# A fused attention and mixer kernel: all tasks put in the order of a precomputed table, the last two weight transfers held behind early loads, batch four's rk by DMA transpose, uT in two tiles

## The chip, the cores and the metric

One Trainium2 chip, one core. The metric is the device time of one execution in microseconds (us). An execution over 1.5% above the fastest of the same kernel is called slow and is left out of ratios. Each kernel was profiled in one execution only, so a trace shows what can happen, not always what happens each time. The profile gives the span from the first to the last instruction, 1.0 to 1.8 us below the time.

Names: PE is TensorE (matmuls and transposes by matmul), ACT is ScalarE, DVE is VectorE, POOL is GpSimd, SP is SyncE, here only a queue that issues transfers. The kernel is written so that each engine takes its instructions in the order in which they were emitted.

## The reference

A linear attention with decay over B=4 batches, H=8 heads, S=768 steps, D=48, then a token and channel mixer:

```python
for t in range(S):                                       # attention, per batch and head
    cur = einsum('bhd,bhe->bhde', u[None] * kt, vt)
    y[:, :, t] = einsum('bhd,bhde->bhe', rt, state + cur)
    state = w[None, :, :, None] * state + einsum('bhd,bhe->bhde', kt, vt)
x = y.transpose(0, 2, 1, 3).reshape(B, S, H * D)         # (4, 768, 384)
h = relu(x.T @ w_tok1) @ w_tok2                          # token mixer, 768 -> 256 -> 768
u = x + h.T
out = u + relu(u @ w_ch1) @ w_ch2                        # channel mixer, 384 -> 1536 -> 384
```

## The kernel before

The 768 steps of a batch are cut into 6 units of 128 steps. A unit goes through: loads of k, r, v (192 KB each, on SP's queue); kp = k times decay, rp = r times decay; transposes of both (rk); scores `at`; masked scores `AT`; state `kv`; output `y`; sum `x_b`. Batch one, for which there is no other work to overlap with, uses an f32 form (`m`, `trk`, `trr`, `mT`, `ad`) with more PE and less POOL work. When a batch's six `x_b` are there, its mixer runs: `hidden`, `back` (u_sb), a transpose of u (uT), 24 `up` steps (z_ps, zr) and 6 `down` steps (h_ps, osb), of which each `up` is 3 matmuls of 384 columns and each `down` 12. The next batch's attention is meant to run beside this batch's mixer.

Order is written out by hand: in batch one slot by slot, later by weaving lists with guessed costs.

```python
def load_unit(b, c):                                   # SP's queue, k then r then v
    for nm, src in (("kt", k), ("rt", r), ("vt", v)):
        ...
        ins = sp.dma_start(dst, src[b, :, ts(c, T), :].rearrange("h s d -> s h d"))
        if (b, c) in after and nm == "kt":             # (1, 0): wait for batch one's last x_b
            tc.add_manual_dep(ins.ins, after[b, c].ins.name, ..., reason="weights first")
...
WEIGHTS_AT = {4: (0,), 5: (1,), 6: (2,), 7: (3, 4)}    # POOL's queue, by slot of batch one;
                                                       # 2 and 3 are the halves of w_ch1, 4 is w_ch2
WARM = (10, 2, 1)                                      # idle_ps matmuls to keep PE's clock up:
                                                       # 10 at the start, then 2 or 1 a slot
...
after[1, 0] = done[0, C - 1]
...                                                    # batch one's mixer beside batch two's attention
items = ups(0, 0, 6) + u1[:6] + downs(0, 0, 0, 1) + u1[6:] + downs(0, 0, 1) + downs(0, 1)
events = [att(0.5, 6), att(4.0, 7)] + [att(8.0 + 3.2 * j, 8 + j) for j in range(7)] + mixing(...)
merge(items, fetch([0.0] * 6 + [12.0, 15.0, 18.0, 22.0, 35.0, 36.5]) + events)
```

rk of batches two to four is turned on PE (8 matmuls into PSUM) and copied by ACT. u of batches two to four is turned by DMA into one tile `uT` of 3 x 768.

Of the kernel before, what the change touches and what calls it, by code (L numbers as in the profile page):

```python
# [18 lines left out]
Ln = ACTF.Ln  # L19


@with_exitstack
def kernel(
# [24 lines left out]
    NJ = dch // 128  # L48

    const = ctx.enter_context(tc.tile_pool(name="const", bufs=1))  # L50
    wts = ctx.enter_context(tc.tile_pool(name="wts", bufs=1))
    lpool = ctx.enter_context(tc.tile_pool(name="lpool", bufs=8))
# [3 lines left out]
    zpool = ctx.enter_context(tc.tile_pool(name="zpool", bufs=2))  # L56
# [4 lines left out]


# [11 lines left out]


    loaded = {}
    done = {}
    after = {}

    rpads = [const.tile([128, H, P], f32, name=f"rpad{c}") for c in range(C)]  # L80

    def load_unit(b, c):
        tiles = []
        for nm, src in (("kt", k), ("rt", r), ("vt", v)):
            if b == 0 and nm == "rt":
                t = rpads[c]
                dst = t[:, :, 0:D]
            else:
                t = lpool.tile([128, dm], f32, name=nm)
                dst = h3(t)  # L90
            ins = sp.dma_start(dst, src[b, :, ts(c, T), :].rearrange("h s d -> s h d"))
            if (b, c) in after and nm == "kt":
                tc.add_manual_dep(ins.ins, after[b, c].ins.name,
                                  mybir.DependencyInfo(mybir.DependencyClass.Sync,
                                                       mybir.DependencyReason.DATA),
                                  reason="weights first")
            tiles.append(t)
        loaded[b, c] = tiles



# [5 lines left out]
    act.dma_start(w_bc, w.rearrange("h d -> (h d)").partition_broadcast(128))  # L107
# [5 lines left out]
    load_unit(0, 0)  # L113
    sp.dma_start(ud, u.rearrange("h d -> (h d)").rearrange("(j p) -> p j", p=128))
    load_unit(0, 1)
# [4 lines left out]
    WARM = (10, 2, 1)  # L120

    def keep_warm(n):

        for _ in range(n):
            z_ps = psM.tile([128, 512], f32, name="idle_ps", tag="m")
            pe.matmul(z_ps, warm[:, 0:128], warm, start=True, stop=True)

# [32 lines left out]
    NB = 3  # L160
    rps = []; kps = []; S0s = []
    for i in range(NB):
        kp_i = const.tile([128, H, P], bf16, name=f"kp{i}")
        dve.memset(kp_i, 0.0)
        kps.append(kp_i)

    keep_warm(WARM[0])
# [5 lines left out]
    wpT = const.tile([128, G, HP, T], f32, name="wpT")  # L173

# [6 lines left out]
    def decay_rT(g):  # L181
        if g == 0:
            for a in range(HP):
                act.activation(wpT[:, g, a, :], steps[:, ts(g, T)], Exp, scale=lnwd[:, a:a + 1])
        else:
            act.activation(wpT[:, g], powers[g - 1], Exp)

    powers = [const.tile([128, HP, T], f32, name=f"powers{g}") for g in range(1, G)]

    def exponents(g):  # L190
        pool.tensor_mul(powers[g - 1], steps[:, ts(g, T)].unsqueeze(1).to_broadcast([128, HP, T]),
                        lnwd.unsqueeze(2).to_broadcast([128, HP, T]))
# [3 lines left out]
    wG = const.tile([128, HP], f32, name="wG")  # L196
    decay_rT(0)
    u_blk = const.tile([128, 3, H], f32, name="u_blk")


    for i in range(2):
        S_i = const.tile([128, HP, 2, D], bf16, name=f"S0_{i}")
        S0s.append(S_i)
    bm = const.tile([128, HP, 2, D], f32, name="bm")
    wGm = const.tile([128, HP, 2, D], f32, name="wGm")


# [8 lines left out]
    def constants_1():  # L216
        pool.tensor_mul(u_blk, heads, ud.unsqueeze(2).to_broadcast([128, 3, H]))

    def constants_2():
        act.activation(wG, lnwd, Exp, scale=float(G * T))  # L220
        pool.tensor_mul(wGm, bm, wG.unsqueeze(2).unsqueeze(3).to_broadcast([128, HP, 2, D]))

    def constants_3():

        for i in range(NB):
            rp_i = const.tile([128, H, P], bf16, name=f"rp{i}")
            dve.memset(rp_i, 0.0)
            rps.append(rp_i)


# [3 lines left out]
    wch2 = wts.tile([128, NJ, dm], bf16, name="wch2")  # L234

    WEIGHTS_AT = {4: (0,), 5: (1,), 6: (2,), 7: (3, 4)}

    def load_weights(which):
        half = ds(0, dch // 2), ds(dch // 2, dch // 2)
        parts = [(wtok1, moe_w_tok1), (wtok2, moe_w_tok2), (wch1[0], moe_w_ch1[:, half[0]]),  # L240
                 (wch1[1], moe_w_ch1[:, half[1]]), (wch2, moe_w_ch2)]
        for i in which:
            t, src = parts[i]
            pool.dma_start(t, src.rearrange("(c p) k -> p c k", p=128))

    x_bs = [xpool.tile([128, C, dm], bf16, name="x_b", bufs=3) for b in range(B)]


    live = {}
    kv = [None]  # L250
    count = [0]

    BY_POOL = (3, 5)

    def stage_p(b, c):

        g = c % G
        kt, rt, vt = loaded.pop((b, c))
        i = count[0] % NB
        count[0] += 1  # L260
        kp = kps[i]
        vb = apool.tile([128, dm], bf16, name="vb", bufs=4)
        L = live[b, c] = dict(kp=kp, vb=vb, rt=rt, vt=vt)
        (dve if b == 0 and c not in BY_POOL else pool).tensor_mul(kp[:, :, 0:D], h3(kt), h3(wn[:, g, :]))
        if b == 0:
            L["m"] = apool.tile([128, dm], f32, name="m", bufs=2)
            pool.tensor_mul(h3(L["m"]), h3(kt), rt[:, :, 0:D])
        if b > 0:
            L["rp"] = rps[i]
            pool.tensor_mul(L["rp"][:, :, 0:D], h3(rt), h3(wp[:, g, :]))  # L270
            L["ku"] = apool.tile([128, dm], f32, name="ku", bufs=2)
            pool.tensor_mul(L["ku"], kt, u_bc)

# [3 lines left out]
    def stage_a(b, c):  # L277

        L = live[b, c]
        rk = L["rk"] = apool.tile([128, 2, HP, T], bf16, name="rk")  # L280
        if b == 0:

            trk = psM.tile([128, HP, T], bf16, name="trk", tag="m")
            trr = psM.tile([128, HP, T], f32, name="trr", tag="m")
            for a in range(HP):
                pe.transpose(trk[:, a, :], pair(L["kp"], a), ident)
            act.copy(rk[:, 0], trk)
            for a in range(HP):
                pe.transpose(trr[:, a, :], pair(L["rt"], a), ident_f)
            dve.tensor_mul(rk[:, 1], trr, wpT[:, c % G])  # L290
            mT_ps = psM.tile([128, 3, T], f32, name="mT_ps", tag="m")
            for j in range(3):
                pe.transpose(mT_ps[:, j, :], L["m"][:, ts(j, 128)], ident_f)
            L["mT"] = apool.tile([128, 3, T], f32, name="mT", bufs=2)
            act.copy(L["mT"], mT_ps)
            act.copy(L["vb"], L["vt"])
            return
        tr_ps = psM.tile([128, 2, HP, T], bf16, name="tr_ps", tag="m")
        for j, src in ((0, L["kp"]), (1, L["rp"])):
            for a in range(HP):  # L300
                pe.transpose(tr_ps[:, j, a, :], pair(src, a), ident)
        act.copy(rk, tr_ps)
        act.copy(L["vb"], L["vt"])

        rku = apool.tile([128, dm], f32, name="rku", bufs=2)
        dve.tensor_mul(rku, L["ku"], L["rt"])
        L["adg"] = apool.tile([128, H], f32, name="adg")
        dve.tensor_reduce(L["adg"], h3(rku), axis=mybir.AxisListType.X, op=ALU.add)

    def own_step(L):  # L310
        L["yd"] = apool.tile([128, dm], f32, name="yd")
        pool.tensor_mul(h3(L["yd"]), h3(L["vb"]), L["adg"].unsqueeze(2).to_broadcast([128, H, D]))

    def stage_b(b, c):

        L = live[b, c]
        rk = L["rk"]
        if b > 0:
            own_step(L)
        at_ps = [psA.tile([128, HP, T], f32, name=f"at_ps{q}", tag=f"at{q}") for q in range(2)]  # L320
        for a in range(HP):
            for q in range(2):
                rows = slice(q * P, q * P + D)
                pe.matmul(at_ps[q][:, a, :], rk[rows, 0, a, :], rk[rows, 1, a, :], start=True, stop=True)
        L["AT"] = []
        for q in range(2):
            AT = apool.tile([128, HP, T], bf16, name=f"AT{q}")
            dve.tensor_mul(AT, at_ps[q], mask.unsqueeze(1).to_broadcast([128, HP, T]))
            L["AT"].append(AT)
        if b == 0:  # L330

            ad_ps = psM.tile([128, H], f32, name="ad_ps", tag="m")
            for j in range(3):
                pe.matmul(ad_ps, L["mT"][:, j, :], u_blk[:, j, :], start=(j == 0), stop=(j == 2))
            L["adg"] = apool.tile([128, H], f32, name="adg")
            act.copy(L["adg"], ad_ps)

    state = {}

    def stage_c(b, c):  # L340
# [253 lines left out]
```

## Time and profile before

| | before |
|---|---|
| time, median of 3 (range) | 185.08 us (184.67 to 185.6) |
| span of the profiled run | 184.1 us |
| PE busy | 165.5 us, 90% |
| POOL, DVE, ACT busy | 93.8, 106.0, 100.0 us |
| PE idle at 40-50 us | 4.5 us |

From the page of the kernel before: the busy tenths of PE, the granted PE clock and the share of the DMA engines in 40 slices of 4.6 us.

```profile
PE 165.5 (90%) x1504; PEld 106.8 (58%) x1504; DVE 106.0 (58%) x193; ACT 100.0 (54%) x217; POOL 93.8 (51%) x113
...
PE   7788888893699899798999999899999999999992
...
PEclk9999999999699999999999999999999999999999
DMA  4999998999999998124699999233011134211212
```

PE has little to give: 18.6 us of idle in all. The one deep hole is in slices 10 and 11 (counted from one). The DMA engines are full from the second to the sixteenth slice (to about 73 us), so in that time a transfer comes earlier only if another comes later.

The same by windows (columns: window, length, busy us and count per engine, granted clock, DMA share, GB/s):

```profile
30.00:40.00 10.00, 9.26 (x74) 5.40 (x72) 5.01 (x12) 5.62 (x14) 0.83 (x1) 1.00 1.15 183
40.00:50.00 10.00, 5.48 (x32) 3.06 (x30) 1.44 (x2) 4.95 (x11) 4.52 (x5) 0.85 1.10 188
50.00:60.00 10.00, 10.00 (x116) 6.77 (x114) 8.11 (x13) 7.93 (x16) 10.00 (x11) 0.98 1.10 220
```

PE is idle for 4.5 us from 40 to 50 us. POOL (the fifth busy figure) has 0.83 us of work from 30 to 40 us, and is full from 50. What they wait for is in the chain of waits that ended last (start, duration, what):

```profile
32.19 14.15 DMA rt<-in_r_dram
46.48 1.00 POOL rp_661 L68
47.52 0.61 PE tr_ps L68 x4
```

A load of 192 KB, which takes 3.9 us in the median of the page's list of transfers, took 14.15 us here, beside two weight transfers in the same 16 engines: the larger one, issued at 28.46 us, landed 17.6 us later at about 46.1, and r at 46.3. The multiply of r and PE's transpose waited for it:

```profile
43.44 0.40 PE L68 MATMUL tr_ps<-ident,kp_139 128*128 128x128 bf16 x4 [0.83 <-POOL kp_139 L68]
47.52 0.61 PE L68 MATMUL tr_ps<-ident,rp_661 128*128 128x128 bf16 x4 [3.69 <-POOL rp_661 L68]
```

### The profile page before, as it was taken

What the parts mean: (1) busy time and instruction counts of PE and PEld (TensorE: products, weight loads), DVE (VectorE), ACT (ScalarE), POOL (GpSimd) and SP (SyncE); (2) the same over time, 40 slices, a digit from 0 to 9 for tenths busy, and PEclk for the clock granted to TensorE, in tenths of its full rate; (3) what the DMA queues carried; (4) which work ended last, traced back from release to release, by engine and by line L of the source; (5) the groups of instructions that cost most, each with busy time, mean ns of one, the idle gap of its engine ahead of it and who ended that gap; (6) DMA issues with size and microseconds to landing.
All of it is one profiled execution on the core that took longest, in us unless ns stands there. A gap on an engine that the chain in (4) does not pass through costs nothing.

```text
span 184.1 us, 3991 instructions
## 1 busy us (share of the span) xinstructions
PE 165.5 (90%) x1504; PEld 106.8 (58%) x1504; DVE 106.0 (58%) x193; ACT 100.0 (54%) x217; POOL 93.8 (51%) x113
## 2 busy tenths in 40 slices
PE   7788888893699899798999999899999999999992
PEld 2376776461367566465667666666665665656651
DVE  6465877700469999974669977996541071121121
ACT  2695565493578744404959748654645444445500
POOL 5459795002999999943597999991100000000000
PEclk9999999999699999999999999999999999999999
DMA  4999998999999998124699999233011134211212
GB/s 92 185 203 163 191 141 143 196 184 196 187 219 215 234 225 195 45 45 107 136 235 232 189 243 196 44 67 108 0 46 43 43 86 89 85 43 43 85 47 85
DMA packets 90354, 24.44 MB, mean 133 GB/s; under 512 B 83680, under 2 KB 90336, under 8 KB 90336
## 3 DMA queue, kind: packets, MB, share of 16 engines
q1 hardware_dynamic: 86368, 20.85, 54.0%
q0 software_dynamic: 3408, 3.15, 11.0%
q10 hardware_dynamic: 560, 0.20, 0.7%
q8 instruction: 12, 0.20, 0.4%
q14 instruction: 6, 0.05, 0.1%
HBM read 20.84 MB, written 4.72 MB: 139 GB/s over the span
## 4 chain that ended last, share of the span: by engine, by line
PE 58%; POOL 14%; DMA 13%; DVE 6%; ACT 5%; issue 3%; ACTq 0%; SPq 0%; DVEq 0%; POOLq 0%
PE h_ps L68 23%; PE z_ps L68 20%; DMA rt<-in_r_dram 8%; POOL ku L68 3%; POOL yd L68 3%; DMA wd<-in_w_dram 3%; PE tr_ps L68 3%; DMA uT<-u_sb 3%; PE y_ps L68 2%; PE ad_ps L68 2%; POOL rp_661 L68 2%; POOL rp_663 L68 1%; PE hT_ps L68 1%; POOL rp_665 L68 1%; DVE u_sb L68 1%
## 5 line engine op out<-in xcount | busy, mean ns | idle before, releaser
L68 ACT ACTIVATE zr<-z_ps 128x384 bf16<-128x384 f32 x96 | 44.3, 495 | 31.7 <-PE z_ps L68 31.6
L68 PE MATMUL h_ps<-wch_198,zr 128*128 128x384 bf16 x288 | 50.4, 326 | 0.2
L68 PEld LDWEIGHTS <-zr 128*128 128x128 bf16 x288 | 28.0, 98 | 18.9 <-issue 1.0
L68 DVE TENSOR_TENSOR osb<-u_sb,h_ps 128x384 f32<-128x384 bf16 x24 | 13.3, 552 | 44.5 <-PE h_ps L68 44.5
L68 ACT COPY rk<-tr_ps 128x1024 bf16<-128x1024 bf16 x18 | 18.2, 1012 | 19.2 <-PE tr_ps L68 18.7
L68 PE MATMUL z_ps<-uT,wch_0_196 128*128 128x384 bf16 x144 | 27.6, 337 | 1.1 <-DMA uT<-u_sb 1.1
L68 PE MATMUL z_ps<-uT,wch_1_197 128*128 128x384 bf16 x144 | 26.5, 326 | 0.8 <-ACT zr L68 0.6
L68 DVE TENSOR_TENSOR rku<-ku,rt 128x384 f32<-128x384 f32 x18 | 18.6, 1033 | 11.3 <-POOL ku L68 11.3
L68 POOL TENSOR_TENSOR yd<-vb,adg 128x384 f32<-128x384 bf16 x24 | 20.0, 834 | 7.3 <-DVE adg L68 6.7
L68 PEld LDWEIGHTS <-wch_0_196 128*128 128x128 bf16 x144 | 14.0, 101 | 10.4 <-issue 3.2
L68 POOL TENSOR_TENSOR ku<-kt,u_bc 128x384 f32<-128x384 f32 x18 | 20.0, 1110 | 0.0
L68 PEld LDWEIGHTS <-wch_1_197 128*128 128x128 bf16 x144 | 13.8, 98 | 10.1 <-issue 1.7
L68 DVE TENSOR_TENSOR x_b<-y_ps,yd 128x384 bf16<-128x384 f32 x24 | 13.3, 553 | 10.6 <-POOL yd L68 5.6
L68 POOL TENSOR_TENSOR kp_139<-kt,wn 128x384 bf16<-128x384 f32 x7 | 7.0, 999 | 17.2 <-DMA kt<-in_k_dram 11.5
L68 PEld LDWEIGHTS <-rk 48*128 48x128 bf16 (+1 forms) x272 | 11.4, 95 | 6.3 <-issue 3.0
L68 DVE TENSOR_TENSOR u_sb<-x_b,hT_ps 128x384 bf16<-128x384 bf16 x24 | 11.8, 547 | 1.5 <-PE hT_ps L68 1.5
L68 ACT CAST vb<-vt 128x384 bf16<-128x384 f32 x24 | 12.3, 514 | 0.0
L68 DVE TENSOR_REDUCE adg<-rku 128x8 f32<-128x384 f32 x18 | 9.9, 553 | 0.8
L68 PE MATMUL hT_ps<-h1r,wtok_195 128*128 128x384 bf16 x48 | 9.4, 326 | 0.9 <-ACT h1r L68 0.8
L68 PE MATMUL idle_ps<-warm 128*128 128x512 bf16 x20 | 7.8, 520 | 2.2 <-DVE warm L68 1.3
L68 PE MATMUL h_ps<-x_b,wtok_194 128*128 128x384 bf16 x48 | 8.9, 325 | 0.1
L68 POOL TENSOR_TENSOR rp_661<-rt,wp 128x384 bf16<-128x384 f32 x6 | 6.6, 1101 | 3.1 <-DMA rt<-in_r_dram 3.1
(318 smaller groups left out, 253.6 us busy)
## 6 DMA issues: line engine op xcount, KB each, us to landing
kt<-in_k_dram SPq DMA_DIRECT2D x24, 192.0 KB, 3.7
vt<-in_v_dram SPq DMA_DIRECT2D x24, 192.0 KB, 3.9
out_dram<-osb SPq DMA_DIRECT2D x24, 192.0 KB, 1.9
rt<-in_r_dram SPq DMA_DIRECT2D x18, 192.0 KB, 3.9
wch_198<-in_moe_w_ch_dram POOLq DMA_DIRECT2D x1, 1152.0 KB, 17.6
wch_0_196<-in_moe_w_ch_dram POOLq DMA_DIRECT2D x1, 576.0 KB, 8.9
wch_1_197<-in_moe_w_ch_dram POOLq DMA_DIRECT2D x1, 576.0 KB, 10.5
wtok_194<-in_moe_w_tok_dram POOLq DMA_DIRECT2D x1, 384.0 KB, 7.5
```

The costliest lines, as they stand in the source:

```text
L68: return lambda *args, **kw: tc.keep_in_program_order(f(*args, **kw))
```

## The change

The intent: a model of engines and queues, run beforehand, searched for an order of all 900-odd tasks of the kernel; its result is a table of numbers, and the kernel emits task after task by it. With it come: batch two's loads from about 20 us on, not held; the two last weight transfers held behind two k loads; batch four's rk by DMA transpose (SP issues it; no PE, no ACT); two units of batch two in the f32 form; two more kp multiplies on DVE; more warm matmuls in batch one; uT in two tiles; deeper buffers for some tiles, and fewer for the loads (8 to 6). The core of the diff (the table, and the functions that only changed their wrapping, are cut):

```diff
+ORDER = [
+    38, 41, 36, 37, 39, 42, 0, 40, 15, 142, 1, 128, 16, 4, 116, 46, 2, 144, 133, 117, 5, 17, 45, 121, 134,
+    ...                                                        # 914 numbers
+]
+    AHEAD = 6; NB = 4; ZB = 3; RK = 4                          # buffers of loads, kp and rp, zr, rk
+    style = ['f32', ... x6, 'pe', 'pe', 'pe', 'pe', 'f32', 'f32', 'pe', ... x6, 'dma', ... x6]
+    DVE_KP = (0, 1, 2, 4, 7, 9,)
+    W_DEP = {3: (1, 1, 0), 4: (1, 2, 0)}                       # weight 3 waits for k of unit (1, 1), ...
...
+        ins = pool.dma_start(t, src.rearrange("(c p) k -> p c k", p=128))
+        if i in W_DEP:
+            tc.add_manual_dep(ins.ins, asked[W_DEP[i]].ins.name, ..., reason="in turn")
...
+            if style[n] == "dma":
+                def turn_rk(j, src):
+                    return lambda: sp.dma_start_transpose(rk_tile()[:, j], src[i].rearrange("p h d -> p (h d)"))
...
-        uT = mpool.tile([128, 3, S], bf16, name="uT")
+            M["uT"] = [mpool.tile([128, 3, S // 2], bf16, name=f"uT{i}") for i in range(2)]
...
-    merge(items, fetch([0.0] * 6 + [12.0, 15.0, 18.0, 22.0, 35.0, 36.5]) + events)
+    plan.run(ORDER)
```

## The prediction

> **What bounds it now.** The page gives TensorE (PE) 90% busy: 165.5 of 184.1 us, so at most 18.6 us of idle can be recovered. By 10 us windows that idle is 2.8 before 10 us, 2.7 from 10 to 30, 0.7 from 30 to 40, 4.5 from 40 to 50, 3.2 from 60 to 90, 0.8 from 110 to 120, and 3.4 at the end. From 120 to 180 us PE is full. Until about 62 us the DMA engines are full too (DMA share 1.0 to 1.15). The 40-50 gap is a transpose waiting 3.7 us for the multiply of batch two's r, whose load was issued at 32.2 us and landed 14.1 us later (chain of waits): batch two's loads are held until batch one is done, then starve behind the weights. From 50 to 74 us the chain runs on POOL (kp, rp, ku, yd, about 4 us a unit).
>
> **What the change does.**
> 1. Loads of batch two go out from about 20 us; the last two weights wait for two k loads. Bytes are unchanged, so DMA stays full: the order changes, not the sum. The Trainium skill ("DMA: Bandwidth & Descriptors", Issuing engines are not separate DMA queues) says all queues share the same 16 engines; the 14.1 us landing agrees.
> 2. Batch four's six units lose their PE transposes (0.55 us a unit, -3.3 us) and 6 ACT copies of 1.01 us; their DMA transposes fall where DMA share is 0.1 to 0.6. Two units of batch two go the f32 way: trk 0.24, trr 0.45, mT 0.33, ad 0.77 instead of 0.55: +2.5 us of PE, -2 us of POOL. Net PE about -1 us. Two kp multiplies move to DVE.
> 3. Warm matmuls in the f32 stage 10 -> 18 (0.22 us each): filler, at worst +1.
> 4. uT in halves: the first ups wait for three transposes, not six.
> 5. The table interleaves finely; queues stay in order, so each error of its model becomes a stall.
>
> **Sum.** Batch one ends at 31.2 us now; I expect 29 to 31. Then 24 ups precede the first down; ACT has about 17.5 us there (24 x 0.46 relu, three 1.0 copies, states, casts) against PE's 15.6, and the last weight lands at about 53 by my count of transfers. So the first down starts at about 54 us (53.0 now, but with 6 fewer ups and 1 to 2 fewer attention units done). PE work left then: downs 46.8, ups 35.1, hidden and back 11.7, transposes 7.5, scores, outputs, states 13.5: 114.6 us; the same count for before is 120.8. With 2% for seams, 2.5 idle and the 3.4 tail, the span is about 176.5.
>
> **Predicted: 177 us, 80% range 172.5 to 182.** Faster by over 2%: 0.84; within 2%: 0.13; slower: 0.03.
>
> **Signs.** PE busy about 165, idle 10 to 13; the 14 us landing gone from the chain; POOL no long run in it; the 40-50 gap 1 to 3 us; ACT near full at 36-54; no PE wait over 1 us for batch four's rk; the end unchanged.
>
> **What would make it wrong.** Batch two's first r, now issued after k of units two and three, starves again and PE waits 4 us or more; the last weight lands after 56 us; DMA transposes on SP's queue delay loads or rk at 110-140 us; a DVE/POOL order that stalls batch one. Better than 172: batch one ending by 27 us.

One number in it is wrong as a reading of the code: 18 warm matmuls are defined, but the table holds only 15 of them (10 in the same stage before).

## The result

| | before | changed |
|---|---|---|
| time, median (range), 4 runs each | 185.19 (184.67 to 185.6) | 179.0 (177.84 to 181.01) |
| ratio of the fast runs | | 0.9634, 95% interval 0.9579 to 0.9688 |
| same chip and rounds | 185.66 (11 runs) | 179.12 (6 runs), ratio 0.9643 (0.960 to 0.9687) |
| span of the profiled run | 184.1 | 177.2 (fast run) |
| PE busy | 165.5, 90% | 163.2, 92% |

Ratios here and below are the mean time of one kernel's fast runs over that of the other's of the same rounds, so they are not quite the ratio of the medians quoted.

The change is 3.6% faster; the predicted 177 us was 2 us low and the range held. The first profile of the changed kernel fell in a slow run (181.0 us), so the lines shown here are of run `c_after`, which is the same file:

> The changed kernel again, unaltered, to have its time on the same chip and rounds as its variants, and a trace in the fast state (the first one was slow at 181.0 us; three others were 177.8 to 179.7). Expected 178 to 179 us, ratio to before 0.963. In the trace: batch one's last x_b at about 34 us against 31.7 before, no idle of PE from 40 to 80 us, and 1 to 3 us of PE idle at 110 to 130 us where batch three's uT and batch four's rk come by DMA.

From its page:

```profile
PE 163.2 (92%) x1479; PEld 105.8 (60%) x1479; DVE 106.4 (60%) x195; ACT 94.5 (53%) x215; POOL 89.6 (51%) x109
...
PE   7579999789999999999899998959899999999991
...
PEclk9996999999999999999999999999999999999999
DMA  4999999999997998965998965559741224400222
```

The hole at slices 10 and 11 is gone. There is a new one at slice 27 (115 to 120 us), and the clock dips in slice 4. By windows:

```profile
30.00:40.00 10.00, 8.31 (x72) 5.29 (x67) 8.77 (x17) 5.90 (x16) 7.04 (x8) 1.00 1.08 192
40.00:50.00 10.00, 10.00 (x92) 6.49 (x90) 4.07 (x8) 9.90 (x25) 6.13 (x7) 1.00 1.24 188
50.00:60.00 10.00, 10.00 (x106) 6.60 (x104) 7.66 (x14) 5.67 (x12) 5.02 (x5) 1.00 0.90 181
110.00:120.00 10.00, 7.98 (x62) 4.61 (x61) 5.98 (x12) 1.52 (x4) 0.30 (x1) 1.00 0.50 124
```

At 30-40 us POOL is now busy for 7.0 us instead of 0.8: batch two's data is there. At 40-60 us PE has no idle at all (4.5 us before), with the DMA engines nearly as full as before; at 60-80 us it has none either (2.3 us before). At 110-120 us 2.0 us of PE are lost (0.8 before). PE waits there for uT, whose transposes SP issued late. PE's timeline, then SP's:

```profile
117.60 1.14 PE L142 MATMUL z_ps<-uT,wch 128*128 128x384 bf16 x6 [2.02 <-DMA uT<-u_sb]
```

```profile
106.65 2.58 SPq L142 DMA_TRANSPOSE rk<-rp  x2
109.39 1.19 SPq L142 DMA_TRANSPOSE rk<-kp  x1
110.68 0.52 SPq L142 DMA_DIRECT2D out_dram<-osb  x1
111.26 1.21 SPq L142 DMA_TRANSPOSE rk<-kp  x1
112.56 5.09 SPq L142 DMA_TRANSPOSE uT<-u_sb  x4
```

Each DMA transpose holds SP's queue for about 1.2 us here. u_sb of four steps was done at 109.4 us, but uT was issued only from 112.6: two of batch four's rk transposes and a store stood in front of it.

Batch one did not get faster. Its last sum, before and now:

```profile
31.19 0.56 DVE L68 TENSOR_TENSOR x_b<-y_ps,yd 128x384 bf16<-128x384 f32 x1 [0.93 <-PE y_ps L68]
```

```profile
32.23 0.56 DVE L142 TENSOR_TENSOR x_b<-y_ps,yd 128x384 bf16<-128x384 f32 x1 [0.51 <-PE y_ps L142]
```

The expectation of `c_after` had put its end at about 34 us; it is 32.8. Four more traces of kernels with the same first hundred tasks have it at 32.20 (`e_rk_pe`), 31.75 (`e_uT_one`) and 31.59 us (`e_late`, `e_uT_first`), so 0.6 us of it changes from execution to execution.

### The profile page after: what moved, and what is told of

It reads as the page before. It is cut to its first block, busy times and chain, and to the rows that moved or that the text cites. A ratio compares the mean times of both kernels' runs of the same rounds, so it can differ in the third digit from the quotient of the medians.

```text
span 179.3 us, 3935 instructions
## 1 busy us (share of the span) xinstructions
PE 163.5 (91%) x1479; PEld 106.0 (59%) x1479; DVE 105.5 (59%) x195; ACT 94.8 (53%) x215; POOL 90.4 (50%) x109
## 3 DMA queue, kind: packets, MB, share of 16 engines
q0 software_dynamic: 3408, 3.15, 11.1%
## 4 chain that ended last, share of the span: by engine, by line
PE 55%; DMA 18%; POOL 8%; issue 5%; SPq 5%; ACT 4%; DVE 3%; POOLq 0%; DVEq 0%
PE h_ps L142 24%; PE z_ps L142 18%; SPq L142 5%; DMA wtok<-in_moe_w_tok_dram 5%; DMA rk<-rp 3%; DMA uT<-u_sb 3%; PE y_ps L142 3%; DMA kt<-in_k_dram 3%; PE at_ps L142 2%; POOL m L142 2%; PE hT_ps L142 2%; DMA ud<-in_u_dram 2%; DMA vt<-in_v_dram 2%; POOL kp L142 2%; POOL yd L142 2%
## 5 line engine op out<-in xcount | busy, mean ns | idle before, releaser
L142 PE MATMUL z_ps<-uT,wch 128*128 128x384 bf16 x288 | 51.0, 326 | 3.6 <-DMA uT<-u_sb 3.2
L142 PE MATMUL h_ps<-wch,zr 128*128 128x384 bf16 x288 | 51.9, 326 | 0.0
L142 PEld LDWEIGHTS <-wch 128*128 128x128 bf16 x288 | 27.2, 98 | 20.9 <-issue 3.9
L142 DVE TENSOR_TENSOR AT<-at_ps,mask 128x512 bf16<-128x512 f32 x48 | 31.4, 682 | 12.4 <-PE at_ps L142 12.4
L142 POOL TENSOR_TENSOR rp<-rt,wp 128x384 bf16<-128x384 f32 x16 | 17.4, 1087 | 7.5 <-DMA rt<-in_r_dram 6.2
L142 POOL TENSOR_TENSOR kp<-kt,wn 128x384 bf16<-128x384 f32 x18 | 18.5, 1030 | 2.5 <-DVE AT L142 1.4
L142 PEld LDWEIGHTS <-kp 128*128 128x128 bf16 x152 | 10.7, 100 | 5.1 <-DVE kp L142 1.5
L142 PEld LDWEIGHTS <-wtok 128*128 128x128 bf16 x96 | 8.9, 98 | 7.9 <-issue 1.4
L142 ACT CAST S<-kv_ps 48x192 bf16<-48x192 f32 x32 | 10.0, 311 | 5.0 <-PE kv_ps L142 4.6
L142 PE MATMUL at_ps<-rk 48*128 48x128 bf16 x192 | 9.7, 222 | 2.2 <-DMA rk<-rp 1.3
L142 PE MATMUL idle_ps<-warm 128*128 128x512 bf16 x25 | 10.3, 508 | 1.3 <-DVE warm L142 1.3
```

Of the source, the lines that this page charges most:

```text
L142: return lambda *args, **kw: tc.keep_in_program_order(f(*args, **kw))
```

## The experiments

Twelve kernels ran, in three calls of four; each call has its own runs of the kernel before (medians 185.66, 185.61, 185.56 us), to which the ratios refer. Each call ran on another chip. Medians and ranges are of all six runs, slow ones too. All gave correct results.

| run | edit | time, median (range), us | ratio to before (95%) |
|---|---|---|---|
| c_after | the change as it is | 179.12 (178.61 to 182.13) | 0.9643 (0.9600 to 0.9687) |
| e_rk_pe | batch four's rk by PE and ACT | 179.01 (178.20 to 180.35) | 0.9652 (0.9610 to 0.9694) |
| e_front | front of the table as before | 180.38 (179.69 to 182.05) | 0.9734 (0.9691 to 0.9777) |
| e_nowarm | no warm matmuls in the table | 181.56 (181.33 to 182.85) | 0.9794 (0.9758 to 0.9830) |
| e_late | old transfer order, new table | 189.41 (188.82 to 190.57) | 1.0203 (1.0166 to 1.0240) |
| b_early | old kernel, loads not held | 183.92 (183.36 to 185.39) | 0.9923 (0.9879 to 0.9966) |
| b_early_held | old kernel, new transfer order | 186.48 (185.96 to 188.57) | 1.0053 (1.0013 to 1.0094) |
| e_warm_early | six late warm matmuls out | 177.94 (177.02 to 179.54) | 0.9592 (0.9545 to 0.9639) |
| e_uT_first | uT ahead of one rk on SP | 177.70 (177.24 to 179.05) | 0.9581 (0.9542 to 0.9620) |
| e_uT_one | uT in one tile | 179.08 (177.72 to 180.59) | 0.9639 (0.9597 to 0.9682) |
| e_best | e_warm_early and e_uT_first | 179.55 (177.82 to 179.96) | 0.9665 (0.9623 to 0.9707) |
| e_best_18pe | e_best, one unit's rk by PE | 177.38 (176.12 to 179.74) | 0.9547 (0.9506 to 0.9587) |

### Where the gain comes from: transfers or order of tasks

**e_late**: the new table with the old rule for the DMA engines.

```diff
-    W_DEP = {3: (1, 1, 0), 4: (1, 2, 0)}
+    W_DEP = {}
+        # kt of (1, 0) waits for batch one's last x_b; the three loads of batch two that stood
+        # before it in the table, and the two last weights, are moved to where they were
```

> The changed kernel with the old DMA order put back and nothing else: batch two's first load waits for batch one's last x_b, and the last two weights are issued without waiting for k loads, in the place they have in the kernel before. Theory A (the gain comes from the order of the transfers: loads of batch two before the last weights): the PE gap of 3.5 to 4.5 us at 40 to 50 us and a landing of over 10 us for batch two's first r are back, total 4 to 6 us slower than the changed kernel, about 183 to 185. Theory B (the gain is from the finer interleave, fewer PE transposes and less POOL work): at most 2 us slower.

Measured 189.41 us, ratio 1.0203: not 4 to 6 but about 10 us slower than the changed kernel, and slower than the kernel before. PE's list of waits (total, times, longest) and ACT's timeline say why it is more:

```profile
PE z_ps L140 <- ACT uT L140: 9.8, 1, 9.8
```

```profile
35.73 0.48 ACT L140 COPY uT<-t_ps 128x384 bf16<-128x384 bf16 x1 [0.42 <-PE t_ps L140]
45.69 0.51 ACT L140 CAST vb<-vt 128x384 bf16<-128x384 f32 x1 [9.48 <-DMA vt<-in_v_dram]
46.11 0.85 ACT L140 COPY uT<-t_ps 128x384 bf16<-128x384 bf16 x2
```

The table puts a cast of batch two's v in the middle of ACT's copies of batch one's uT, since by its model v has landed. With the old transfers it has not; ACT, in order, stands for 9.5 us before a cast that nobody needs yet, and the whole mixer stands with it. So the table holds the arrival of the data in itself: it is a bad order for any other arrival. The run shows that the new order needs the new transfers. It does not show that the transfers alone are the gain, and the next two test that.

**b_early**: the kernel before, with the hold taken away.

```diff
-    after[1, 0] = done[0, C - 1]
```

> The kernel before with one thing taken away: batch two's loads no longer wait for batch one's last x_b, so SP issues them from about 21 us; weights as before. Theory A (the order of transfers is the gain, and lifting the hold is its main part): no PE wait over 1.5 us at 40 to 50 us, total 3 to 5 us faster than before, 180 to 182. Rival (the weights' queue takes the engines from 26 us on whatever SP has issued, so holding the weights is needed too): the gap shrinks only in part, 0 to 2.5 us faster.

Measured 183.92 us, ratio 0.9923: the rival's 0 to 2.5 us. The wait moves one unit on. The chain of waits:

```profile
27.62 20.11 DMA rt<-in_r_dram
...
47.87 0.07 POOL rp L68
```

The second unit's r, issued at 27.6 us, landed 20.1 us later; the last weights were issued at 27.6 us too. The Trainium skill, "DMA: Bandwidth & Descriptors", Queues, rings and completion order, says that each engine takes turns between the queues by packet. SP's packets are small (rows of 48 floats, 192 bytes) and the weights' larger (3.15 MB in 3408 packets), so turns by packet, if the page means the packets that the profile counts, would leave SP the smaller part; the 20.1 us here and the 14.15 us in the kernel before agree with that, but no run changed the size of the packets.

**b_early_held**: the kernel before with the whole transfer order of the change: no hold for the loads, a hold for the last two weights.

```diff
-    WEIGHTS_AT = {4: (0,), 5: (1,), 6: (2,), 7: (3, 4)}
+    WEIGHTS_AT = {4: (0,), 5: (1,), 6: (2,), 7: ()}
+            if i > 2:
+                tc.add_manual_dep(ins.ins, asked[1, i - 2, "kt"].ins.name, ..., reason="in turn")
-    after[1, 0] = done[0, C - 1]
+    load_next(3)
+    load_weights((3, 4))
```

> The kernel before with the whole transfer order of the change and nothing else of it: batch two's loads are not held (as in b_early, 1.4 us faster than before, where r of its second unit, issued at 27.6 us, landed only at 47.7), and the last two weights are issued after batch one, the first when k of batch two's unit 1, the second when k of its unit 2 has landed. Theory A (the change's gain is the order of the transfers): no wait of PE over 1.5 us at 40 to 55 us, r of unit 1 landing in under 10 us, 3 to 6 us faster than before, 179.5 to 182.5. Rival (the old order of tasks, with POOL at about 4 us a unit on the chain from 50 to 74 us, cannot use earlier data): the wait moves to a later place, under 2.5 us faster than before.

Measured 186.48 us, ratio 1.0053: no gain at all. Theory A falls, and the rival's reason (POOL) is not the main one either: PE's waits for POOL's rp are 1.3 us in all, its wait for a weight is 6.1. (The trace is of the slowest of the six runs, 188.57 us.) POOL's timeline, and PE's:

```profile
36.63 0.80 POOL L68 DMA_DIRECT2D wch<-in_moe_w_ch_dram  x1 [6.07 <-DMA kt<-in_k_dram]
39.63 1.05 POOL L68 DMA_DIRECT2D wch<-in_moe_w_ch_dram  x1 [2.20 <-DMA kt<-in_k_dram]
```

```profile
45.49 5.93 PE L68 MATMUL z_ps<-uT,wch 128*128 128x384 bf16 x18 [6.13 <-DMA wch<-in_moe_w_ch_dram]
```

The second half of w_ch1 is now issued at 36.6 us, and PE, which in the old order asks for it after six `up` steps, waits 6.1 us. The changed kernel issues it no earlier to speak of:

```profile
35.65 0.80 POOL L142 DMA_DIRECT2D wch<-in_moe_w_ch_dram  x1 [1.66 <-DMA kt<-in_k_dram]
```

but has twelve `up` steps that need only the first half, comes to the thirteenth at about 44.5 us, and does not stop there. So the three runs say: new order with old transfers 1.020, old order with new transfers 1.005, old order with half of the new transfers 0.992, both new 0.964. The gain belongs to neither alone. That at 40-50 us it comes from moving batch two's loads before the weights and, at the same time, putting the work that needs the weights later, is what the waits say; it is not shown by a run, since none took the old order with the first twelve `up` steps alone changed. The 2.3 us of idle gone at 60-80 us, where PE mostly waited for POOL's rp before, were not tested apart from the rest of the new order.

### Batch one

**e_nowarm**: the warm matmuls taken out of the table (15 of them; the text says 18).

```diff
-    ... 15, 142, 1, 128, 16, 4, ...
+    ... 142, 1, 128, 4, ...            # 15 to 27, 31 and 32 are gone
```

> The 18 warm matmuls of the f32 stage are taken out of the table; the 10 at the very start stay. Theory A (they only fill waits and keep the clock up): granted clock falls in more of 8 to 30 us and batch one ends up to 2 us later, total 0 to 2 us slower. Theory B (PE is in order, so each of them, 0.22 us or more, stands ahead of real work): batch one ends 1 to 2 us earlier, total 1 to 2 us faster.

Measured 181.56 us, ratio 0.9794 against 0.9643: 1.6% slower, more than theory A allowed, and theory B falls. By windows, first without the warm matmuls, then the changed kernel:

```profile
14.00:16.00 2.00, 2.00 (x20) 1.94 (x21) 0.55 (x1) 1.15 (x4) 1.19 (x2) 0.50 1.36 187
18.00:20.00 2.00, 2.00 (x11) 2.00 (x11) 0.95 (x3) 0.17 (x1) 1.05 (x2) 0.50 1.36 192
20.00:22.00 2.00, 2.00 (x19) 1.94 (x18) 1.47 (x3) 0.59 (x2) 2.00 (x3) 0.50 1.17 174
22.00:24.00 2.00, 2.00 (x33) 1.85 (x31) 1.65 (x4) 1.54 (x5) 1.32 (x2) 0.99 0.69 116
```

```profile
14.00:16.00 2.00, 2.00 (x20) 1.74 (x19) 0.08 (x1) 1.40 (x4) 2.00 (x3) 0.50 1.40 199
18.00:20.00 2.00, 1.94 (x21) 1.57 (x20) 2.00 (x5) 0.57 (x2) 1.84 (x2) 1.00 1.47 169
20.00:22.00 2.00, 2.00 (x36) 1.86 (x34) 1.57 (x4) 1.57 (x4) 2.00 (x3) 1.00 1.37 213
```

Third from the end of each line is the granted clock. Without the warm matmuls it stays at 0.50 from 8.4 to 22 us, although PE is shown busy for all of the windows 14-16 and 18-22. The work of that stage is transposes and small matmuls (8 to 128 columns). The Trainium skill, "TensorE: Matmul & The Clock Gate", Part 4: PE-mode transpose, says of transposes that they do not count as PE-busy in the same way. The run agrees in part: the clock is 0.50 at 18-20 us, where eight transposes of r take most of the 2.00 us busy of 2.00; but it is back at 22.1 us with no warm matmul, after 4.9 us without idle of PE, over half of them transposes.

In the changed kernel the clock falls too, at 13.3 us, and is back at 16.7. This differs between executions: it does not fall there in the traces of `e_rk_pe`, `e_late` and `e_uT_first`, which have the same tasks and warm matmuls up to then. But all six runs of `e_nowarm` have a mean clock of 0.953 to 0.962, all six of `c_after` 0.981 to 0.991 (the trace of `e_nowarm` is of its slowest run, 182.85 us, with the lowest). The 15 warm matmuls of 512 columns together are thus not filler. Why the clock comes back when it does stays open.

**e_warm_early**: only the six warm matmuls after 17.5 us taken out.

```diff
-    ... 148, 24, 150, ... 165, 25, 188, ... 203, 26, 177, ... 111, 27, 194, 31, 208, ... 178, 32, 209, ...
+    ... 148, 150, ... 165, 188, ... 203, 177, ... 111, 194, 208, ... 178, 209, ...
```

> Of the 15 warm matmuls that the table really holds in the f32 stage (the text of e_nowarm said 18), the six after 17.5 us are taken out: in the trace of the changed kernel PE has no idle from 20 to 31 us and they lie on the chain of waits, 1.3 us. Theory A: granted clock stays as it was, batch one's last x_b 1 us earlier, total 0.7 to 1.3 us faster. Rival (they too keep the clock, or the time freed becomes a wait for DVE or for the first weight): total within 0.5 us, or slower.

Measured 177.94 us, ratio 0.9592. Batch one's last sum starts at 30.98 us instead of 32.23:

```profile
30.98 0.56 DVE L140 TENSOR_TENSOR x_b<-y_ps,yd 128x384 bf16<-128x384 f32 x1 [0.51 <-PE y_ps L140]
```

In the chain of waits of c_after the six stand with 1.3 us. Against the five traces that have them (31.59 to 32.23 us) the gain is 0.6 to 1.2 us. The mean clock of the runs did not fall (0.987 to 1.000), so the clock did not need these six. The interval of the ratio overlaps that of c_after, so the total is only likely, not shown, to be lower.

**e_front**: the first 44 places of the table in the order of the kernel before.

```diff
-    38, 41, 36, 37, 39, 42, 0, 40, 15, 142, 1, 128, 16, 4, 116, ...
+    36, 37, 38, 39, 40, 41, 42, 116, 119, 117, 121, 123, 2, 120, 124, 125, 0, ...
```

> Only the first tasks of the table are put in the order of the kernel before (loads k, r, v of unit 0 then of unit 1; POOL multiplies m before the exponents; ACT copies rk of unit 0 before the decay tables of groups 1 and 2). Theory A (the table's front makes batch one late: first scores at 12.4 us against 10.0, and the delay is carried to its end): first scores at about 10 us, last x_b of batch one at about 32 us instead of 34.3, and 1.5 to 2.5 us less in all. Theory B (batch one's end does not matter because the weights of the second mixer layer and batch two's loads come from full DMA engines whatever the order): batch one earlier, PE then waits at 40 to 56 us, total within 0.7 us.

Measured 180.38 us, ratio 0.9734: slower, so both theories fail as stated. The first scores did come at 10.3 us, but the rest ran at half clock (six of the ten us from 10 to 20):

```profile
10.00:16.00 6.00, 6.00 (x34) 4.38 (x34) 1.98 (x3) 4.03 (x11) 2.83 (x3) 0.50 1.17 198
```

and batch one's last sum started at 33.3 us. The edit changed the places of the warm matmuls along with the rest, so the run says nothing clean about the order of the front. Nor is the clock the whole reason that it is slower: the one run whose mean clock was 0.998 took 180.03 us, against 178.6 to 179.3 of the fast runs of c_after.

### Batch four's rk and SP's queue

**e_rk_pe**: rk of batch four turned by PE and copied by ACT.

```diff
-    style = [..., 'dma', 'dma', 'dma', 'dma', 'dma', 'dma']
+    style = [..., 'pe', 'pe', 'pe', 'pe', 'pe', 'pe']
+    # the two tasks of each unit keep their numbers, and are moved to up to 16 places before its scores
```

> Batch four's rk turned on PE and copied by ACT, as for batches two and three; all else as in the changed kernel. Theory A (the DMA transposes save their 3.3 us of PE, as the change intends): 1.5 to 3 us slower than the changed kernel. Theory B (what they save on PE they give back: SP's queue is held about 1.2 us by each of the 12, so loads and batch three's uT start later and PE waits 2 to 3 us at 110 to 130 us): within 0.7 us of it, with those waits gone from the list of waits of PE.

Measured 179.01 us, ratio 0.9652 against 0.9643: theory B. PE is busy for 167.2 us instead of 163.2 (some records can be missing; 6 x 0.55 would be 3.3) in a span of 177.3 instead of 177.2. PE's list of waits, changed kernel first:

```profile
PE z_ps L142 <- DMA uT<-u_sb: 2.6, 2, 2.0
...
PE at_ps L142 <- DMA rk<-rp: 1.0, 2, 0.8
```

```profile
PE z_ps L140 <- DMA uT<-u_sb: 1.0, 2, 0.6
```

What the DMA transposes save on PE is given back as waits for uT and rk: 3.6 us in c_after, 1.0 here.

**e_uT_first**: one number of the table moved, so that SP issues batch three's uT before one rk transpose that is needed much later.

```diff
-    ... 761, 519, 509, ... 767, 790, 469, ...      # 519 = DMA transpose of kp, batch four, fourth unit
+    ... 761, 509, ... 767, 790, 519, 469, ...      # now after the fourth uT transpose of batch three
```

> One task moved: the DMA transpose of kp of batch four's unit 4, which SP issues just ahead of batch three's uT, is issued after the first four uT transposes; its scores come 20 us later. Theory A (SP's in-order queue is what makes uT late): uT is issued 1.2 us earlier, PE's longest wait for uT (2.0 us at about 117 us) falls to about 0.8, total 0.7 to 1.3 us faster. Theory B (uT's own transfers or the PE order set it): the wait stays.

Measured 177.70 us, ratio 0.9581. PE's waits for uT fall from 2.6 to 1.4 us in all, the longest from 2.0 to 0.9. PE's list of waits, and from its timeline the step that waited 2.02 us in c_after:

```profile
PE z_ps L140 <- DMA uT<-u_sb: 1.4, 2, 0.9
```

```profile
115.69 1.14 PE L140 MATMUL z_ps<-uT,wch 128*128 128x384 bf16 x6 [0.39 <-DVE AT L140]
```

This is theory A, and more than it: the wait for batch three's uT was to fall to about 0.8 us and is gone. The 0.9 us that are left are another wait, for batch two's uT at 80.8 us, which the edit does not touch. The total fell by 0.6% in ratio, about 1.1 us, with overlapping intervals. A part of that may be the clock of batch one, which did not dip in this trace (its last sum came at 31.59 us, 0.6 earlier than in c_after).

**e_uT_one**: uT in one tile.

```diff
-            M["uT"] = [mpool.tile([128, 3, S // 2], bf16, name=f"uT{i}") for i in range(2)]
+            uT1 = mpool.tile([128, 3, S], bf16, name="uT")
+            M["uT"] = [uT1[:, :, ds(i * (S // 2), S // 2)] for i in range(2)]
```

> The changed kernel with uT in one tile of 768 columns as before, all else the same. Theory (two tiles let the first ups wait for three DMA transposes only): PE's waits for uT grow from 2.6 us in all to 5 us or more, total 1 to 3 us slower than the changed kernel's ratio of 0.964. Rival (the tracking goes by parts of a tile, or other work fills in): within 0.7 us.

Measured 179.08 us, ratio 0.9639: no difference. The waits for uT are 3.5 us in all against 2.6, the longest 2.0 in both; the one that c_after has not, 0.8 us at 81.7, is also in e_uT_first with two tiles (0.9 at 80.8). Two tiles are worth nothing measurable here. Whether that is because dependencies are followed by parts of a tile, or because the later halves arrive in time anyway, the run does not tell.

### A better version

**e_best** joins e_warm_early and e_uT_first.

> Both edits that helped, together: without the six late warm matmuls (alone ratio 0.9592 to before, against 0.9643 of the changed kernel) and with batch three's uT ahead of one rk transpose on SP (alone 0.9581). If they add, as they sit in different stages: ratio 0.953 to 0.955, about 176.5 to 177 us. If the later stage swallows the first edit: 0.957 to 0.960.

Measured 179.55 us, ratio 0.9665: the gains do not add; there is no gain at all over c_after. Batch one ends at 30.98 us as in e_warm_early, but at 80 us the lead is gone:

```profile
80.92 1.62 PE L140 MATMUL z_ps<-uT,wch 128*128 128x384 bf16 x9 [1.48 <-DMA uT<-u_sb]
```

PE waits 1.5 us there for batch two's uT, where the changed kernel did not wait, and 1.3 us at 110 us for an rk. The edits do not cause the wait at 80 us: up to about 108 us the table is the same, number for number, as that of e_warm_early, whose trace has no such wait. So it is a difference between executions (or chips). Why e_best should be slower than either edit alone is not settled; the ranges of the three overlap (177.8 to 180.0, 177.0 to 179.5, 177.2 to 179.1 us), but the interval of the ratio just clears that of e_uT_first (0.9623 against 0.9620).

**e_best_18pe** takes e_best and turns rk of batch four's first unit on PE.

```diff
-    style = [..., 'dma', 'dma', 'dma', 'dma', 'dma', 'dma']
+    style = [..., 'pe', 'dma', 'dma', 'dma', 'dma', 'dma']
```

> As e_best, and rk of batch four's first unit goes by PE and ACT instead of two DMA transposes, which frees SP for 2.4 us just ahead of batch three's uT. If SP's queue is still what makes uT late there, PE's wait for uT at 110 to 120 us is under 0.3 us and the total 0.3 to 1 us below e_best; if not, 0 to 0.6 us above it for the added 0.55 us of PE.

Measured 177.38 us, ratio 0.9547 (0.9506 to 0.9587), the lowest ratio: 1% below the changed kernel, with intervals that do not overlap, and a span of 175.1 us. From e_uT_first and e_warm_early it is not told apart; their intervals overlap with its own. PE does not wait for uT at 110-120 us; its waits for uT are 1.4 us in all, none over 0.8. The expectation on that wait holds but decides nothing, since e_best does not wait there for uT either. What fell is the wait at 110 us for an rk, from 1.3 to 0.2 us, and the one at 80 us, from 1.5 to 0.8. That the total is 2 us below e_best, for one unit, is more than the 0.3 to 1 us expected, and carries the doubt about e_best with it.

## Why the prediction was right, and where not

The time was right: 177 predicted, 179.0 measured, faster by 6.2 us where 8 were forecast. The span of 176.5 us was nearer still to the 177.2 of the fast profile. The two halves of the sum held as well: the first `down` at 54 us against 53.5, and from there 122.8 us (114.6, 2% for seams, 2.5, 3.4) against 123.7. Inside them some terms erred and cancelled, and that is luck:

- **"The 40-50 gap is a transpose waiting for batch two's r"**: right, and that is where most of the gain is; PE's idle at 40-60 us went from 4.5 to 0 us. The prediction left 1 to 3 us there, too little gain. It counted the transfers correctly ("the order changes, not the sum"), but named only the order of the transfers for this gap. The runs show that this is not enough: b_early_held (1.005) and e_late (1.020) each have half of it and lose.
- **"The first down starts at about 54 us"**: 53.5 in the fast profile. The last weight, issued at 37.4 us, landed 13.9 us later, at 51.3; about 53 had been counted.
- **"Batch one: I expect 29 to 31"**: its last sum started at 32.2 us and not at 31.2; wrong, by 1 to 3 us. It cost nothing in the sum, since the first `down` came on time. Step 3 explains 0.6 to 1.2 us of it; the rest is not settled.
- **"Warm matmuls ... filler, at worst +1"** (step 3): about right in size for what was added, wrong as a view of what they are. The six late ones cost batch one 0.6 to 1.2 us. All 15 together are worth 2.8 us (181.74 against 178.95, means of fast runs), with a clock of a half for 13.7 us without them against 3.4 us with them in the two traces. No run has 10 of them, as before, in the new table.
- **"Net PE about -1 us"**: busy PE went from 165.5 to 163.2 us, and its idle from 18.6 to 14.0 (10 to 13 expected). But the 3.3 us that batch four's transposes save are paid back: e_rk_pe takes the same time.
- **"No PE wait over 1 us for batch four's rk"**: right by the letter (0.8). What the sign did not name was uT: SP's queue, held by rk transposes, made PE wait 2.0 us for it. The prediction listed SP's queue as something that could go wrong, and put nothing for it into the sum.
- **"2.5 us idle" after the first down**: it was 4.3 us (0.6 at 80-90, 0.8 at 100-110, 2.0 at 110-120, 0.9 at 120-130, from the windows of c_after). This is the mis-sized term for the later stage, and the 2% for seams (2.3 us) made up for it.
- **"uT in halves"**: no effect (e_uT_one). The 0.9 us wait at 80-90 us is still 0.6.
- **"Each error of its model becomes a stall"**: e_late, where the arrivals were changed on purpose, shows it at full size, 9.5 us for one cast.

Still open: why e_best is no faster than its parts, when the clock of batch one falls and returns, and how fast batch one could be with its front reordered and the clock kept up.

## What to carry to other kernels

When DMA engines are full, moving one transfer forward delays another; here it gave at most 0.8% until the work that needs the displaced transfer was moved back too. Change both together, and judge neither by itself. An order computed from expected arrivals is an order for these arrivals only: on in-order engines, one early place for a task whose data comes late stops everything behind it. Before moving work from a busy engine to a DMA queue, look at what else that queue has to issue in the same microseconds, and before deleting matmuls that "do nothing", look at the clock.

## What the Trainium skill lacked or had wrong

- "TensorE: Matmul & The Clock Gate", Part 4, says that transposes do not count as busy for the clock in the same way. It has no case of a mix of transposes and matmuls of 8 to 128 columns. Here such a mix, busy for 2.00 of 2.00 us at 14-16 and 18-22 us, left the clock at 0.50 from 8.4 to 22 us (e_nowarm); but the clock was back at 22.1 us after 4.9 us of the same mix without idle.
- "DMA: Bandwidth & Descriptors", Queues, rings and completion order, says that queues take turns by packet, but not what that does to a queue of small packets: 192 KB in 192-byte packets landed after 14.15 us (before) and 20.11 us (b_early) beside weight transfers, against a median of 3.9 us (before).
- "DMA: Bandwidth & Descriptors", DMA Transpose (X-bar), gives no time for which a transpose holds the queue that issues it; the page has issue times of transposes only in a table about trn3, with a column for earlier generations, and none for this size. Here, SBUF to SBUF, 128 x 512 of 2 bytes held SP's queue for about 1.2 us each (1.19 and 1.21 us in c_after).
